# Weight sums of a Strassen stage: first set split in place, eight PSUM banks in the stage before, sums moved behind the maxima

## The chip, the cores and the metric

The kernel runs on one core of one Trainium2 chip. The metric is the device time of one execution in microseconds. Three runs of the kernel before gave 671.41, 668.84 and 676.40 us, median 671.41 us. The profile shown here is of one further execution, which took 672.27 us; its span, from the first to the last instruction, is 670.5 us, so 1.77 us of it lie outside the span.

## The reference

Three blocks follow each other: a retention attention over 4 x 8 heads, a mixture of 8 experts with top-1 routing, and a feed-forward block whose hidden layer is the maximum of three projections. The change touches only the last:

```python
def _moe2_ref(x, w1, w2, w3, w_out):          # x: 2304 x 512, w1..w3: 512 x 768, w_out: 768 x 512
    h = np.maximum(np.maximum(x @ w1, x @ w2), x @ w3)
    return (h @ w_out).astype(np.float32)
```

All data is fp32. Each product is computed as three matmuls on operands split into a high part (rounded to the fp32r format) and a low part (the rest): high x high, high x low, low x high.

## The kernel before, in words

The attention and the experts come first (0 to about 370 us). What matters here is the last block. Its input lies in SBUF as `y` (128 partitions, 4 chunks of the model dimension, 2304 tokens and a pad of 352 columns behind them). The tokens are cut into six tiles of 384. The hidden dimension is cut into six blocks of 128 (`f`). Weight unit `8E + 2f` holds w1 and w2 of a block, the next unit holds w3 and w_out, each split into high and low, in SBUF.

**The first pair of token tiles (i = 0, 1)** is done directly. `up(i, f)` runs twelve times, in the order f = 0: i = 0, 1; f = 1: i = 0, 1; and so on; call s = 2f + i. One call is three PSUM tiles (128 x 384, one each for w1, w2, w3) of twelve matmuls (L1096 to L1098). ACT copies the first tile out (L1267), DVE takes the maximum with the second (L1269) and the third (L1270), ACT rounds the result to the high part (L1271), and DVE subtracts to get the low part (L1273). A tile's bank can be written again when its reader is done. `mm_tile` hands out six banks in turn (four `mm`, and `u` and `o`), so a call's tiles take the banks of the call two before. `up` takes three callbacks: `beside[0]` is called between L1267 and L1269, `beside[1]` between L1271 and L1273, `beside[2]` behind L1273. In calls 0 to 7 they carry the decoding of the last third of the weights, which arrive as packed 64-bit words: ACT L1008 and L1009, DVE L1023 to L1037, POOL L1040 and L1041, a store to the DRAM buffer `wdec` from POOL's queue (L1043), and one step later the split into the unit (ACT L1066, DVE L1067). `down(i)` (L1454 to L1456) then multiplies the hidden tiles by w_out, three row blocks (`r`) of six `f` each; `send` copies a finished block out on ACT (L1434) and scatters it to the output from POOL's queue (L1436). `beside_down` calls a table of steps (`during`) when a row block is finished.

**The other two pairs (i = 2, 4)** use a Strassen-Winograd form of a 2 x 2 block product: seven products in place of eight, for each pair of hidden blocks (`g` = 0 to 2) and each of w1, w2, w3 (`j` = 0 to 2), so nine groups a pair of tiles (`group(q, g, j)`, q = 0 to 17). A group is seven products of six matmuls (L1470). Four of its products use sums of weight quarters, S1 to S4, as the stationary operand; the others use the weights themselves. The four sums of a group are a *set* k = 3g + j. A set is made once, during the first pair and the first groups, by these steps: `gen_load` (SP: two DMAs of 256 KB from `wdec`, L1327), `gen_sums` (DVE: four subtractions or additions of 128 x 256, L1341), `gen_high` (ACT: the high parts, one instruction of 128 x 1024, L1345), `gen_low` (DVE: the low parts, 128 x 1024, L1349, and then two stores of 512 KB to the DRAM tile `sd[k]` from SP's queue, L1353 to L1358). Where a set is worked on is its *home*: for k < 6 one of three regions of `y` whose tokens (columns 0 to 767) are already used, from set 6 on buffers of the pool `rpool`, three in number, which the output rows of `send` use as well.

The groups read the sums from nine *strips*, which are free quarters of weight units that the first pair no longer needs (`strip(n)`). `stream` loads the next strip from `sd` (SP, 256 KB, L1373); five are asked for ahead (`AHEAD`), and each group asks for four more, one behind each product that uses a strip. `form(i)` makes the right-hand operands b11, b12, b21, b22, t1 to t4 of a pair in eleven pieces of work on DVE (L1393 splits, L1398 differences) and ACT (L1386); `work(m)` does the next m of them.

The program is written in manual order: each engine executes its instructions in the order of the code, each DMA queue issues in order, and a step waits in its queue for the data it needs and for the readers of what it overwrites. The tables `gens` (steps during the `up` calls, keyed by call and callback), `during` (row blocks of `down`) and `amid` (places in the first groups) set where the steps of the sets stand in that order.

## Time and profile before

| | |
|---|---|
| three runs | 668.84, 671.41, 676.40 us |
| profiled execution | 672.27 us, span 670.5 us, mean granted TensorE clock 0.98 |
| PE busy, PEld busy | 638.2 us (95%), 598.1 us (89%) |
| DVE, ACT, POOL busy | 443.2 (66%), 275.8 (41%), 207.4 us (31%) |
| twelve `up` calls | up to 450.5 us |
| `down` of the first pair | 450.5 to 475.0 us |
| first nine groups | 475.0 to 547.1 us |

The span is the time between the first and the last instruction; times in the trace count from its start. PEld is the load of a matmul's stationary operand; a gap in PEld is where TensorE's instruction stream really stands, since the ends of pipelined matmuls are modelled. In a row with `<-`, the name behind the arrow is what ended the wait. The granted clock is 1.00 for 2.4 GHz and 0.50 for 1.2 GHz.

### The profile page before, as it was taken

How to read it: one execution, taken by the hardware profiler on the slowest of the kernel's cores; microseconds unless marked ns; L12 is line 12 of the kernel's file. 1: busy time of each engine (PE TensorE's matmuls, PEld its weight loads, DVE VectorE, ACT ScalarE, POOL GpSimd, SP SyncE). 2: the span in 40 equal slices, each digit the busy share in tenths (PEclk: the TensorE clock that was granted, in tenths of full speed). 3: DMA queues.
4: the chain of work that ended last, by engine and by line, in shares of the span. 5: the costliest groups of instructions: out<-in, count | busy, mean ns of one | idle time of the engine just before them, and what ended most of it. 6: DMA issues, size and time to landing. Idle time of an engine off the chain costs nothing.

```text
span 670.5 us, 12025 instructions
## 1 busy us (share of the span) xinstructions
PE 638.2 (95%) x4523; PEld 598.1 (89%) x4523; DVE 443.2 (66%) x866; ACT 275.8 (41%) x501; POOL 207.4 (31%) x184
## 2 busy tenths in 40 slices
PE   8999998899999999999999999999989999999994
PEld 6888877799999989898889999988889998999983
DVE  3488788455858676778877556676767677456630
ACT  3245434244645554665565533323512216211221
POOL 1001113056574644278774054511200002100011
PEclk9999989699999999999999999999989999999998
DMA  8989942335877777677865233357787641444011
GB/s 287 315 255 322 348 123 91 108 108 173 248 198 219 212 228 206 218 240 240 250 219 179 94 95 114 123 205 268 247 280 267 217 149 48 157 141 144 30 47 49
DMA packets 70548, 125.10 MB, mean 187 GB/s; under 512 B 18538, under 2 KB 41966, under 8 KB 70488
## 3 DMA queue, kind: packets, MB, share of 16 engines
q1 hardware_dynamic: 52888, 96.72, 45.3%
q0 software_dynamic: 15200, 23.45, 11.3%
q10 hardware_dynamic: 2400, 4.14, 1.7%
q8 instruction: 37, 0.61, 0.4%
q14 instruction: 23, 0.19, 0.1%
HBM read 98.32 MB, written 25.91 MB: 185 GB/s over the span
## 4 chain that ended last, share of the span: by engine, by line
PE 57%; DMA 16%; DVE 10%; issue 6%; ACT 5%; POOL 4%; ACTq 1%; SPq 0%; POOLq 0%; DVEq 0%
PE s L1470 18%; PE b L1136 10%; DMA raw<-in_weights_dram 5%; PE a L1096 3%; PE a L1098 3%; PE a L1097 3%; PE d L1456 2%; PE d L1454 2%; PE d L1455 2%; DMA wdec<-y 2%; DMA kv<-in_kv_dram 2%; DVE w L148 2%; PE xps L490 2%; DMA xr<-xd,who 1%; PE u L1096 1%
## 5 line engine op out<-in xcount | busy, mean ns | idle before, releaser
L148 DVE TENSOR_TENSOR w<-raw,w 128x1024 fp32r<-128x1024 f32 x72 | 102.0, 1418 | 45.7 <-ACT w L143 45.6
L1136 PE MATMUL b<-h,w 128*128 128x336 f32 (+7 forms) x768 | 118.7, 307 | 3.8 <-ACT h L1112 1.9
L1136 PEld LDWEIGHTS b<-h,w 128*128 128x128 f32 x768 | 109.1, 188 | 6.7 <-DVE h L1113 3.1
L143 ACT ACTIVATE w<-raw 128x1024 fp32r<-128x1024 f32 x72 | 75.9, 1055 | 29.7 <-DMA raw<-in_weights_dram 27.1
L1436 POOL DMA_INDIRECT out_dram<-o,perm_sb x18 | 20.5, 1137 | 206.3 <-ACT o L1434 165.5
L1096 PE MATMUL a<-xt,w 128*128 128x336 f32 (+7 forms) x256 | 78.7, 307 | 0.0
L1098 PE MATMUL a<-xt,w 128*128 128x336 f32 (+7 forms) x256 | 78.4, 306 | 0.0
L1097 PE MATMUL a<-xt,w 128*128 128x336 f32 (+7 forms) x256 | 78.3, 306 | 0.0
L186 POOL DMA_INDIRECT who_d<-tok,slots_i x20 | 21.0, 1050 | 95.0 <-DMA who_d<-tok,slots_i 57.6
L1096 PEld LDWEIGHTS a<-xt,w 128*128 128x128 f32 x256 | 49.1, 192 | 0.4 <-ACT xt L194 0.4
L1097 PEld LDWEIGHTS a<-xt,w 128*128 128x128 f32 x256 | 49.1, 192 | 0.0
L1098 PEld LDWEIGHTS a<-xt,w 128*128 128x128 f32 x256 | 49.0, 191 | 0.0
L173 POOL DMA_INDIRECT xr<-xd,who x24 | 37.5, 1562 | 33.2 <-DVE order_w L1157 20.9
L1096 PE MATMUL u<-ys,w 128*128 128x384 f32 x126 | 43.0, 341 | 2.8 <-ACT m L1267 1.7
L1470 PE MATMUL s<-b_ys,w 128*128 128x384 f32 x216 | 42.3, 344 | 0.2 <-ACT p L1500 0.2
L1098 PE MATMUL u<-ys,w 128*128 128x384 f32 x126 | 42.2, 335 | 0.0
L1097 PE MATMUL u<-ys,w 128*128 128x384 f32 x126 | 42.1, 335 | 0.0
L1470 PE MATMUL s<-b_xt,w 128*128 128x384 f32 x216 | 40.4, 334 | 0.0
L1470 PE MATMUL s<-b_h,w 128*128 128x384 f32 x216 | 40.4, 334 | 0.0
L1470 PEld LDWEIGHTS s<-b_ys,w 128*128 128x128 f32 x216 | 39.2, 195 | 0.7 <-ACT p L1500 0.5
L1112 ACT ACTIVATE h<-a 128x336 fp32r<-128x336 f32 (+7 forms) x64 | 26.4, 423 | 30.6 <-PE a L1098 26.9
L1040 POOL TENSOR_TENSOR d<-d,top 128x512 f32<-128x512 f32 x16 | 21.4, 1339 | 53.5 <-issue 19.7
(282 smaller groups left out, 1334.9 us busy)
## 6 DMA issues: line engine op xcount, KB each, us to landing
raw<-in_weights_dram SPq DMA_DIRECT2D x64, 512.0 KB, 5.2
w<-sd SPq DMA_DIRECT2D x72, 256.0 KB, 4.0
kv<-in_kv_dram SPq DMA_DIRECT2D x16, 512.0 KB, 6.5
qk<-in_qk_dram SPq DMA_DIRECT2D x15, 512.0 KB, 8.4
d<-in_weights_dram POOLq DMA_DIRECT2D x14, 512.0 KB, 5.7
sd<-y SPq DMA_DIRECT2D x12, 512.0 KB, 2.9
wdec<-mag POOLq DMA_DIRECT2D x16, 256.0 KB, 2.9
raw<-wdec SPq DMA_DIRECT2D x8, 512.0 KB, 3.7
```

What stands on the lines that cost most here:

```text
L143: act.activation(out=t[:, 0], in_=raws[w], func=AF.Copy)
L148: engine.tensor_tensor(out=t[:, 1], in0=raws.pop(w), in1=t[:, 0].bitcast(F32), op=ALU.subtract)
L173: pool.indirect_dma_start(out=xr[:n, r, :], out_offset=None, in_=xd[:, :], in_offset=bass.IndirectOffsetOnAxis(ap=who[:n, r, e : e + 1] if ...
L186: pool.indirect_dma_start(out=who_d[:, :], out_offset=bass.IndirectOffsetOnAxis(ap=slots_i[:L, t : t + 1], axis=0), in_=tok[:L, t : t + 1] ...
L1040: pool.tensor_tensor(out=low, in0=low, in1=top.bitcast(F32), op=ALU.mult)
L1096: pe.matmul(ps, lhsT=wh, rhs=xh, start=first, stop=False)
L1097: pe.matmul(ps, lhsT=wh, rhs=xl, start=False, stop=False)
L1098: pe.matmul(ps, lhsT=wl, rhs=xh, start=False, stop=last)
L1112: act.activation(out=h[:, 0, :wide], in_=ps, func=AF.Relu)
L1136: pe.matmul(ps, lhsT=w[:, a, f * P : (f + 1) * P], rhs=hs[f][:, b, :wide], start=(i == 0), stop=(i == len(todo) - 1),)
L1436: pool.indirect_dma_start(out=out[:, :], out_offset=bass.IndirectOffsetOnAxis(ap=perm_sb[:, g : g + 1], axis=0), in_=o, in_offset=None,)
L1470: pe.matmul(ps, lhsT=a[:, k], rhs=b[:, c], start=first and c == 0 and n == 0, stop=c == 1 and n == 2, skip_group_check=True,)
```

## The change

The `up` calls take their PSUM tiles from `any_tile`, which hands out all eight banks in turn (the two `sc` banks are new to them). Set 0 is no longer stored to DRAM and loaded again: `first_set` writes the high parts of its four sums straight into strips 0 to 3 (ACT, four of 128 x 256), then the low parts (DVE, four of 128 x 256), and `stream` skips set 0 in the first pair. For the second pair its strips are stored to `sd[0]` by four DMAs from POOL's queue. The steps of the sets move: sums that stood between the copy and the maxima of a call (`beside[0]`) stand behind the call's low part (`beside[2]`), right before the set's high and low steps. The homes are written as a table; set 6, and the high half of set 7, use `y`, among it the pad. A set's high half is stored right behind its ACT step, no longer behind the low step. The load of set 6 stands before the last pieces of `work`, that of set 7 later by one group, that of set 8 earlier by two products.

```diff
--- before.py
+++ after.py
@@ -1251,9 +1251,20 @@
         for n in (NSOON, NSOON + 1):
             dec_load(n)
 
+        bank = {"n": 0}
+
+        def any_tile(cols, name):
+            n = bank["n"] % 8
+            bank["n"] += 1
+            if n < 4:
+                return ps_m.tile([P, DM], F32, tag="mm", name=name)[:, :cols]
+            if n < 6:
+                return ps_s.tile([P, DM], F32, tag="uo"[n - 4], name=name)[:, :cols]
+            return side_tile(cols, name)
+
         def up(i, f, m, h, beside=(lambda: None,) * 3):
             wa, wb = units[8 * E + 2 * f], units[8 * E + 2 * f + 1]
-            pss = [mm_tile(TILE2, f"u{i}_{f}_{j}") for j in range(3)]
+            pss = [any_tile(TILE2, f"u{i}_{f}_{j}") for j in range(3)]
             order = [(j, c) for j in range(3) for c in range(NC)]
             if i == 0 and f == 0:
                 order.sort(key=lambda jc: jc[1])
@@ -1308,13 +1319,22 @@
             y[:, :2, span[0]].rearrange("p a (b c) -> p a b c", b=2),
             y[:, 2:, span[0]].rearrange("p a (b c) -> p a b c", b=2),
             y[:, :, span[1]].rearrange(quarters, a=2),
+            y[:, :, NTOK : NTOK + KH].rearrange(quarters, a=2),
         ]
+
+        rooms_of = {(0, 1): 0, (1, 1): 1, (2, 1): 0, (3, 1): 2, (4, 1): 1, (5, 1): 0, (6, 1): 3}
+        rooms_of.update({(1, 0): 2, (2, 0): 1, (3, 0): 0, (4, 0): 2, (5, 0): 1, (6, 0): 1, (7, 0): 3})
+
+        def stored(n):
+            if n < 2:
+                return y[:, 2 * n : 2 * n + 2, span[0]]
+            return y[:, :, span[1]] if n == 2 else y[:, :, NTOK : NTOK + KH]
         S2, S4, S3, S1 = (0, 0), (0, 1), (1, 0), (1, 1)
         gen_t = {}
 
         def gen_tile(k, low):
-            if k < NHOME:
-                return homes[(k + 2 * (1 - low)) % 3]
+            if (k, low) in rooms_of:
+                return homes[rooms_of[k, low]]
             t = rpool.tile([P, 1024], F32, tag="raw", name=f"sum{k}_{low}")
             return t.rearrange("p (a b c) -> p a b c", a=2, b=2)
 
@@ -1340,22 +1360,34 @@
             ):
                 dve.tensor_tensor(out=at(out_), in0=at(a), in1=at(b), op=op)
 
+        def gen_store(k, low):
+            to, t, n = sd[k][:, low], gen_t[k, low], rooms_of.get((k, low))
+            if n is None:
+                sp.dma_start(out=to.rearrange("p a b -> p (a b)"), in_=t.rearrange("p a b c -> p (a b c)"))
+            elif n < 2:
+                sp.dma_start(out=to.rearrange("p (a b) c -> p a (b c)", a=2), in_=stored(n))
+            else:
+                sp.dma_start(out=to, in_=stored(n))
+
+        def first_set(low):
+            for n, (a, b) in enumerate(USE):
+                src, to = gen_t[0, 1][:, a, b], strip(n)
+                if low == 0:
+                    act.activation(out=to[:, 0], in_=src, func=AF.Copy)
+                elif low == 1:
+                    dve.tensor_tensor(out=to[:, 1], in0=src, in1=to[:, 0].bitcast(F32), op=ALU.subtract)
+                else:
+                    pool.dma_start(out=sd[0][:, :, 2 * a + b], in_=to.bitcast(F32))
+
         def gen_high(k):
             t = gen_t[k, 0] = gen_tile(k, 0)
             act.activation(out=t.bitcast(F32R), in_=gen_t[k, 1], func=AF.Copy)
+            gen_store(k, 0)
 
         def gen_low(k):
-            low, high = gen_t.pop((k, 1)), gen_t.pop((k, 0))
-            dve.tensor_tensor(out=low.bitcast(F32R), in0=low, in1=high, op=ALU.subtract)
-            for half, n in ((0, (k + 2) % 3), (1, k % 3)):
-                to, t = sd[k][:, half], (high, low)[half]
-                if k >= NHOME:
-                    sp.dma_start(out=to.rearrange("p a b -> p (a b)"), in_=t.rearrange("p a b c -> p (a b c)"))
-                elif n == 2:
-                    sp.dma_start(out=to, in_=y[:, :, span[1]])
-                else:
-                    to = to.rearrange("p (a b) c -> p a (b c)", a=2)
-                    sp.dma_start(out=to, in_=y[:, 2 * n : 2 * n + 2, span[0]])
+            low = gen_t[k, 1]
+            dve.tensor_tensor(out=low.bitcast(F32R), in0=low, in1=gen_t[k, 0], op=ALU.subtract)
+            gen_store(k, 1)
 
         def strip(n):
             w, j = units[8 * E + 2 * (2 * (n // 3) + 1) + n % 3 // 2], n % 3 % 2
@@ -1368,7 +1400,7 @@
             q = streamed["n"]
             streamed["n"] += 1
             k, use = divmod(q, len(USE))
-            if k < 2 * len(sd):
+            if 0 < k < 2 * len(sd):
                 a, b = USE[use]
                 sp.dma_start(out=strip(q % NRING).bitcast(F32), in_=sd[k % len(sd)][:, :, 2 * a + b])
 
@@ -1418,16 +1450,6 @@
             ]
 
         big = {}
-        bank = {"n": 0}
-
-        def any_tile(cols, name):
-            n = bank["n"] % 8
-            bank["n"] += 1
-            if n < 4:
-                return ps_m.tile([P, DM], F32, tag="mm", name=name)[:, :cols]
-            if n < 6:
-                return ps_s.tile([P, DM], F32, tag="uo"[n - 4], name=name)[:, :cols]
-            return side_tile(cols, name)
 
         def send(i, r, ps):
             o = rpool.tile([P, 1024], F32, tag="raw", name=f"o{i}_{r}")[:, :DM]
@@ -1529,15 +1551,13 @@
             h2[i] += [new_h(i, f) for f in range(2, NFF)]
         gens = {
             (7, 2): [(gen_load, 0)],
-            (8, 0): [(gen_sums, 0)],
             (8, 1): [(gen_load, 1)],
-            (8, 2): [(gen_high, 0), (gen_low, 0)],
-            (9, 0): [(gen_sums, 1), (gen_load, 2)],
-            (9, 2): [(gen_high, 1), (gen_low, 1)],
-            (10, 0): [(gen_sums, 2), (gen_load, 3)],
-            (10, 2): [(gen_high, 2), (gen_low, 2)],
-            (11, 0): [(gen_sums, 3), (gen_load, 4)],
-            (11, 2): [(gen_high, 3), (gen_low, 3)],
+            (8, 2): [(gen_sums, 0), (first_set, 0), (first_set, 1), (gen_load, 2)],
+            (9, 2): [(gen_sums, 1), (gen_high, 1), (gen_low, 1), (first_set, 2)],
+            (10, 0): [(gen_load, 3)],
+            (10, 2): [(gen_sums, 2), (gen_high, 2), (gen_low, 2)],
+            (11, 0): [(gen_load, 4)],
+            (11, 2): [(gen_sums, 3), (gen_high, 3), (gen_low, 3)],
         }
 
         def steps(s, at):
@@ -1571,12 +1591,12 @@
 
         R3 = range(TILE2 // P)
         during = {
-            (0, 0): [(gen_sums, 4), (work, 1), (gen_load, 5)],
-            (0, 1): [(gen_high, 4), (gen_low, 4), (work, 2)],
-            (0, 2): [(gen_sums, 5), (work, 2)] + [(stream, ())] * AHEAD,
-            (1, 0): [(work, 2), (gen_high, 5), (gen_low, 5)],
-            (1, 1): [(work, 1)],
-            (1, 2): [(gen_load, 6)],
+            (0, 0): [(work, 2), (gen_load, 5)],
+            (0, 1): [(gen_sums, 4), (work, 2)],
+            (0, 2): [(gen_high, 4), (work, 1), (gen_low, 4)] + [(stream, ())] * AHEAD,
+            (1, 0): [(gen_sums, 5), (work, 2), (gen_load, 6)],
+            (1, 1): [(gen_high, 5), (work, 1), (gen_low, 5)],
+            (1, 2): [],
         }
 
         def beside_down(i):
@@ -1606,11 +1626,10 @@
         h_f += [halves(y[:, c, : 2 * TILE2]) for c in range(NC)]
         h_f += [halves(y[:, c, 2 * TILE2 : 4 * TILE2]) for c in range(2, NC)]
         amid = {
-            (0, 2): [(gen_sums, 6), (gen_load, 7)],
+            (0, 2): [(gen_sums, 6)],
             (1, 1): [(gen_high, 6)],
-            (1, 2): [(gen_low, 6)],
-            (2, 2): [(gen_sums, 7)],
-            (3, 0): [(gen_load, 8)],
+            (1, 2): [(gen_low, 6), (gen_load, 7)],
+            (2, 2): [(gen_sums, 7), (gen_load, 8)],
             (3, 1): [(gen_high, 7)],
             (3, 2): [(gen_low, 7)],
             (4, 2): [(gen_sums, 8)],
```

On DVE at call 8 (f = 4, i = 0; `m` and `y` are the running maximum, `u` the PSUM tiles, `w` a weight unit, `h` a hidden tile) the order before is:

```order
L1341 TENSOR_TENSOR y<-y 128x256 x4
L1269 TENSOR_TENSOR m_4_5107<-u_4_1_5109,m_4_5107 128x384
L1270 TENSOR_TENSOR m_4_5107<-u_4_2_5110,m_4_5107 128x384
L1067 TENSOR_TENSOR w_5091<-y,w_5091 128x512
L1273 TENSOR_TENSOR h_4_4649<-m_4_5107,h_4_4649 128x384
L1349 TENSOR_TENSOR y<-y 128x2x512
L1341 TENSOR_TENSOR y<-y 128x256 x4
L1269 TENSOR_TENSOR y<-u_4_1_5165,y 128x2x192
L1270 TENSOR_TENSOR y<-u_4_2_5166,y 128x2x192
L1273 TENSOR_TENSOR h_4_4653<-y,h_4_4653 128x384
L1349 TENSOR_TENSOR y<-y 128x2x512
```

and now:

```order
L1280 TENSOR_TENSOR m_4_5107<-u_4_1_5109,m_4_5107 128x384
L1281 TENSOR_TENSOR m_4_5107<-u_4_2_5110,m_4_5107 128x384
L1067 TENSOR_TENSOR w_5091<-y,w_5091 128x512
L1284 TENSOR_TENSOR h_4_4649<-m_4_5107,h_4_4649 128x384
L1361 TENSOR_TENSOR y<-y 128x256 x4
L1378 TENSOR_TENSOR w_4469<-y,w_4469 128x256 x2
L1378 TENSOR_TENSOR w_4516<-y,w_4516 128x256
L1378 TENSOR_TENSOR w_4615<-y,w_4615 128x256
L1280 TENSOR_TENSOR y<-u_4_1_5171,y 128x2x192
L1281 TENSOR_TENSOR y<-u_4_2_5172,y 128x2x192
L1284 TENSOR_TENSOR h_4_4653<-y,h_4_4653 128x384
L1361 TENSOR_TENSOR y<-y 128x256 x4
```

The four sums (L1341, now L1361) moved from ahead of the two maxima to behind the low part, and the four subtractions of `first_set` (L1378) stand in the place of the one large low step of set 0 (L1349).

On SP's queue, at the end of the first pair (`w` are strips, `sd_4636` is `sd[0]`, `sd_4637` is `sd[1]`, and so on), the order before is:

```order
L1373 DMA w_4469<-sd_4636 128x2x256 x2
L1373 DMA w_4516<-sd_4636 128x2x256
L1373 DMA w_4615<-sd_4636 128x2x256
L1373 DMA w_4615<-sd_4637 128x2x256
L1358 DMA sd_4641<-y 128x2x512
L1355 DMA sd_4641<-y 128x4x256
L1327 DMA sum_1_5507<-wdec 128x512 x2
L1373 DMA w_4618<-sd_4637 128x2x256
```

and now:

```order
L1405 DMA w_4615<-sd_4637 128x2x256
L1347 DMA y<-wdec 128x2x256 x2
L1368 DMA sd_4641<-y 128x2x512 x2
L1405 DMA w_4618<-sd_4637 128x2x256
```

The four loads of set 0's strips are gone, and the load of set 6 (L1327, now L1347) has moved from behind to ahead of the two stores of set 5; the next strip of set 1 (`w_4618`, strip 5) still stands behind both stores.

## Rows read from the trace of the kernel before

**Rows 1.** Waits of PEld from 360 us on: total us, times, longest us.

```profile
PEld s L1470 <- DMA w<-sd: 4.5, 2, 4.2
PEld u L1096 <- ACT m L1267: 2.3, 2, 1.4
PEld u L1096 <- DVE y L1269: 1.0, 1, 1.0
PEld u L1096 <- ACT y L1267: 1.0, 4, 0.3
PEld u L1096 <- DVE m L1269: 0.7, 1, 0.7
```

**Rows 2.** Timeline of PE: start us, busy us, engine, line, operation [idle before].

```profile
450.53 0.39 PE L1454 MATMUL d<-w,early_h 128*128 128x512 f32 x1
...
475.05 2.27 PE L1470 MATMUL s<-b_xt,w 128*128 128x384 f32 x12
...
489.01 1.33 PE L1470 MATMUL s<-b_xr,w 128*128 128x384 f32 x6 [3.92 <-DMA w<-sd]
...
496.10 2.24 PE L1470 MATMUL s<-b_xt,w 128*128 128x384 f32 x12
```

**Rows 3.** Windows: busy us of each engine, then granted clock, DMA share, GB/s.

```profile
409.00:411.00 2.00, 1.24 (x7) 1.24 (x8) 1.15 (x3) 1.24 (x4) 1.17 (x2) 1.00 0.14 39
...
491.00:492.00 1.00, 1.00 (x4) 1.00 (x4) 0.01 (x1) 0.00 (x0) 0.00 (x0) 0.50 0.85 262
```

**Rows 4.** Timeline of ACT.

```profile
429.30 0.48 ACT L1267 ACTIVATE y<-u 128x384 f32<-128x384 f32 x1
...
447.31 1.05 ACT L1345 ACTIVATE y<-y 128x1024 fp32r<-128x1024 f32 x1
```

**Rows 5.** Timeline of DVE.

```profile
435.03 3.25 DVE L1341 TENSOR_TENSOR y<-y 128x256 f32<-128x256 f32 x4 [0.58 <-DMA y<-wdec]
...
443.91 1.80 DVE L1341 TENSOR_TENSOR y<-y 128x256 f32<-128x256 f32 x4
445.63 0.55 DVE L1269 TENSOR_TENSOR y<-u,y 128x384 f32<-128x384 f32 x1
...
447.44 0.56 DVE L1273 TENSOR_TENSOR h<-y,h 128x384 fp32r<-128x384 f32 x1 [0.59 <-ACT h L1271]
448.39 1.23 DVE L1349 TENSOR_TENSOR y<-y 128x1024 fp32r<-128x1024 f32 x1 [0.39 <-ACT y L1345]
...
462.56 0.95 DVE L1393 TENSOR_TENSOR b_xt<-y,b_xt 128x768 fp32r<-128x768 f32 x1
```

**Rows 6.** Timeline of POOL and DVE around the last decode steps.

```profile
430.63 0.75 POOL L1043 DMA_DIRECT2D wdec<-y  x1 [0.30 <-DVE y L1269]
431.04 0.69 DVE L1067 TENSOR_TENSOR w<-y,w 128x512 fp32r<-128x512 f32 x1
...
435.70 1.37 POOL L1041 TENSOR_TENSOR y<-y 128x512 f32<-128x512 f32 x1
...
439.33 0.68 DVE L1067 TENSOR_TENSOR w<-y,w 128x512 fp32r<-128x512 f32 x1
```

**Rows 7.** Timeline of SP's queue (issue times).

```profile
479.48 0.36 SPq L1355 DMA_DIRECT2D sd<-y  x1
483.37 0.81 SPq L1327 DMA_DIRECT2D sum<-wdec  x2
484.23 2.58 SPq L1373 DMA_DIRECT2D w<-sd  x4
```

**Rows 8.** The chain that ended last: start us, us, what.

```profile
449.64 2.88 DMA sd<-y
...
460.95 4.81 DMA sd<-y
...
484.23 4.74 DMA w<-sd
```

**Rows 9.** All strip loads, L1373 (72 of them).

```profile
DMA to landing us min/median/max: 3.0/4.0/5.7
```

## The prediction

> **What bounds the kernel now.** I read the share of busy time first: PE issues almost all the time, so only its gaps can be won. The waits of PEld in the stretch that the change touches name them [rows 1]: 5.0 us in the `up` calls (2.3 + 1.0 + 1.0 + 0.7), where a call waits for a bank that ACT's copy or DVE's maximum of the call two before has not freed, and one of 4.2 us in the groups, for a strip. The windows show what the second costs beside the wait [rows 3]: behind those 4.2 us the granted clock is 0.50, that is 1.2 GHz; around the gap of 1.4 us at 409 us it stays at 1.00. From the strip's arrival at 489.01 to the next group at 496.10 [rows 2] are 7.1 us for five products; twelve matmuls take 2.24 with the last one's overhang, about 0.174 each, so a product of six is 1.04 and five are 5.2: clock, and 0.2 of waiting for one more strip, cost 1.9. Behind 496 us I find no gap that the change can touch.
>
> The chain says why the strip was late: SP's queue is in order [rows 7]. The load of set 6 waited for an output buffer until 483.37, the strip behind it was issued at 484.23 and landed 4.74 us later [rows 8].
>
> **The change, part by part.**
>
> *Eight banks.* A call's third tile now waits for the copy (L1267) of the call two before, and its first two tiles for the maxima of the call three before; that is two tiles, 4.2 us, more slack. The copies are held by the decode steps, which do not depend on PE and keep their times. The tightest case is the third tile of call 9. Without gaps the last `up` matmul ends at 450.5 - 5.0 = 445.5; two calls of 6.25 (36 matmuls) and a tile of 2.1 before that is 430.9, and the copy of call 7 is done at 429.8 [rows 4]: 1.1 us to spare. So `up` ends at **445.5**, 5.0 us earlier.
>
> *DVE's queue takes it back in part.* From the end of POOL's last decode step at 437.07 [rows 6] DVE is the longest queue, and I add it up, each step to the start of the next.
> - The rest of call 8 (ACT's split 0.65, DVE's 0.68, the low part 0.5) to 438.95.
> - Sums of set 0, 1.72 (443.91 to 445.63 [rows 5]; the 3.25 of the first row there ran beside POOL's last two arithmetic steps, which are over by then), to 440.7.
> - ACT's four copies of 128x256: the size is not in the trace. One lies between nothing and the 0.48 of 128x384 [rows 4]; I take 0.42, nearer to the upper row. Three run beside the sums and the last beside DVE's first subtraction; without that cover the four cost 1.7.
> - Four subtractions of 128x256: between 0.43, a sum of that size (1.72 / 4), and the 0.68 of 128x512 [rows 6]. I take 0.45, as the size is the sum's; the upper end is 0.9 more in all. To 442.5.
> - Per call, maxima and low part: 2.3 (445.63 to 447.44, and 0.47 [rows 5]). Per set: sums 1.8, ACT's high part 1.05 [rows 4] and 0.1 to hand over, low part 1.15: 4.1. Before, the maxima stood between sums and high part and hid most of ACT's 1.05 (0.39 was left [rows 5]); now DVE waits it out. That is what moving the sums behind the maxima costs.
> - So: call 9 to 444.8, set 1 to 448.9, call 10 to 451.2, set 2 to 455.3, call 11 to 457.5, set 3 to 461.6.
> - Then what `during` holds: seven splits at 0.88 and four differences at 0.96 (0.95 for one [rows 5], less or more by the overlap at the start), sums of sets 4 and 5 at 1.72, their low parts at 1.15, a wait of 0.2 for ACT: 16.0. DVE is through set 5 at **477.6**; before, the last store of set 5 was issued at 479.48 [rows 7].
>
> *PE behind it.* `down` reads the high part of call 10 in its sixth step, at 445.5 + 15 matmuls of 0.227 (108 of them from 450.53 to 475.05 [rows 2]) = 448.9. It is there 1.8 us after the first maximum of call 10 (447.44 less 445.63), at 450.65. PE waits 1.75. The groups start at 445.5 + 1.75 + 24.5 = **471.75** (475.05 before). Their operand t2 is split by 474.7 and its low part first read at 475.05: 0.3 to spare.
>
> *Set 0 in place.* Four strip loads and the wait for them fall away. Its four stores go to POOL's queue, idle until the first output row, and are read 18 groups later. The load of set 6 no longer waits for an output buffer.
>
> *The strip that was late.* Strip 5 belongs to the tenth product, at 471.75 + 9 x 1.04 = 481.1. On SP it stands behind the stores of set 5, so it is issued when DVE is through, at 477.6 + 0.45, and with its 4.74 us of before [rows 8] it is there at **482.8**: PE waits 1.7 us instead of 4.2. The ends are 3.0 and 5.7 [rows 9]; I take the row of the same strip, behind the same store. A wait of this length leaves the clock alone, as at 409 us.
>
> By the fit of the Trainium skill's page "DMA: Bandwidth & Descriptors" (section "Anatomy of one DMA"), 2.0 us and the bytes at 436 GB/s, 256 KB would be there in an estimated 2.6 us. No strip load here was that fast [rows 9]; by it the wait would vanish and the time fall by 1.7 us more.
>
> *Later strips.* Strip 13 now stands behind the low half of set 6 and the load of set 7. DVE's work in group 1 (some 8.2 us from 482.2) and the two issues (0.4 and 0.8) let it go at 491.6; with 4.74 it lands at 496.3 and is read at 482.8 + 5 x 1.04 + 7.3 + 2.1 = 497.4. About 1 us is left: the thinnest cover in the plan.
>
> **Sum.** Strip 5's product starts at 482.8 instead of 489.0: 6.2. No slow clock: 1.9, less 0.2 for the strip behind it. Together **7.9 us**. The profiled execution would take 672.27 - 7.9 = 664.4; the median of the runs shown lies 0.86 below that execution, so I predict 671.41 - 7.9 = **663.5**.
>
> **Rivals.**
> - *Stores held by the DMA engines.* ACT's high step of a set overwrites the home whose store was issued one set earlier. One store landed in 2.88 us, one took 4.81 [rows 8], and POOL's 1 MB now comes on top at 442. At 4.81 throughout, set 2's high part is 0.9 late, set 3's 1.8, later ones no more; and the strip takes 5.7 for 4.74. 2.8 less gain: 666.3. For it: a DMA share of 0.85 at 491 us [rows 3]. Against: the stretch held as many stores and loads before. Chance 0.14.
> - *POOL's stores block DVE.* A split on DVE took 0.69 while POOL issued a store, 0.68 alone [rows 6]: no blocking. If it did block, four issues of 0.75 put 3.0 us on DVE's queue: 666.5. Chance 0.05. The Trainium skill's page "SBUF — State Buffer" (section "SBUF: two separate sides") has a shared port pair, an exclusive lock between a GpSimd instruction that reads SBUF and a DVE instruction with two SBUF inputs; the sums' 3.25 beside POOL's arithmetic would be such a lock, and the pair of rows says that a DMA issue is not.
> - *The wait comes back at strips 13 and 17 (slower).* They stand behind set 6's low half and set 7's load, and behind set 8's load. If one is more than 1.1 us late, and misses by as much as strip 5 did before, it costs 4.2 and 1.9 for the clock, 6.1: 669.6. If both do, 12.2: **675.7**, slower than before. For: SP is in order and 1 us is little. Against: one store and one load of 0.5 MB stand there, and none waits for an output row. Chances 0.06 and 0.04.
> - *DVE's queue is shorter or the strip faster.* If the strip lands in 3.0, PE hardly waits for it: 661.9. If the sets never hold PE, strip 5's product starts at 445.5 + 24.5 + 9.4 = 479.4, and the gain is 9.6 + 1.9 = 11.5: 659.9. Chance 0.12.
>
> **Numbers.** My forecast, 663.5 within 2 us, has the remaining 0.59. The range 659.8 to 669.0 goes from the last rival's end to nearly the single late strip, with the dear subtractions (0.9), the strip's landing and the scatter of the runs inside. A measurement of this kernel can tell about 1% (6.7 us) from no change. Below 664.7: most of the forecast (0.43), the last rival (0.12), a little of the first (0.03): 0.58. Above 678.1: two late strips in a bad run, and what I have not seen: 0.05. Between: 0.37.
>
> **What would show it.** Right: no PEld wait in `up` above 0.3 us; the first `down` matmul near 445.5, with one wait of 1 to 2 us at its sixth step; the last store of set 5 issued near 477.6; a wait of 1 to 2 us in group 1 for a strip, the granted clock 1.00 from 480 to 500. Wrong: waits for banks left in `up` (then the banks were not the limit); stores landing in over 4 us with ACT's high steps waiting for them; a wait for a strip in groups 3 to 5 with the clock at 0.50; or the groups starting at 474 or later, which would mean that DVE's queue took back the whole gain.

## The result, and the profile after

The changed kernel takes 666.07 us, median of 22 runs (660.70 to 671.14), against 672.42 us for the kernel before on the same chip: ratio 0.9903, 95% interval 0.9876 to 0.9931. That is 6.35 us less (4.6 to 8.3 by the interval); 7.9 had been forecast. The ratio leaves out runs more than 1.5% above the fastest of their kernel, so it is not quite the quotient of the two medians. The profiled execution took 667.22 us.

The runs are a blunt measure here: the first `up` matmul, before which the change has no instruction of its own, starts between 365.2 and 377.2 us in the 14 profiles of this study. So I also compare the **stretch** from the first `up` matmul to the last matmul of the program: 661.49 - 370.82 = 290.67 us before, 656.75 - 374.09 = 282.66 us after, 8.0 less. Timeline of PE after (start us, busy us, engine, line, operation, [idle before <- what ended it]):

```profile
374.09 0.34 PE L1096 MATMUL u<-ys,w 128*128 128x384 f32 x1
...
448.98 0.39 PE L1476 MATMUL d<-w,early_h 128*128 128x512 f32 x1
...
453.30 0.50 PE L1476 MATMUL d<-w,h 128*128 128x512 f32 x1 [0.72 <-ACT h L1282]
...
474.66 0.33 PE L1492 MATMUL s<-b_xt,w 128*128 128x384 f32 x1
...
480.55 0.44 PE L1492 MATMUL s<-b_ys,w 128*128 128x384 f32 x1 [1.54 <-ACT p L1522]
...
656.75 0.39 PE L1478 MATMUL d<-w,b_h 128*128 128x512 f32 x1
```

`up` takes 74.89 us (79.71 before), `down` 25.68 (24.52), the rest 182.09 (186.44): -4.8, +1.2, -4.3. The waits of PEld from 360 us on, beside [rows 1] of before:

```profile
PEld s L1492 <- ACT p L1522: 1.9, 1, 1.9
PEld d L1476 <- ACT h L1282: 1.1, 1, 1.1
PEld s L1492 <- DMA w<-sd: 0.4, 1, 0.4
PEld d L1478 <- DVE h L1284: 0.3, 1, 0.3
```

The 5.0 us for banks are gone and so are the 4.2 us for strip 5. The last row but one is not strip 5 but strip 13, two groups later (timeline of PEld):

```profile
500.65 1.00 PEld L1492 LDWEIGHTS s<-b_xr,w 128*128 128x128 f32 x6 [0.38 <-DMA w<-sd]
```

New are 1.4 us at call 10's hidden tile (1.14 for the high part, 0.30 for the low). In group 0, `p` is late by 1.9 us: it is ACT's copy of the group's first product, and the fifth product is added to the same bank. The kernel before has a wait there too, of 0.5 us, which [rows 1] leave out (PEld):

```profile
479.59 1.00 PEld L1470 LDWEIGHTS s<-b_ys,w 128*128 128x128 f32 x6 [0.51 <-ACT p L1500]
```

ACT, DVE, SP and the chain tell why `p` is late now. ACT:

```profile
469.61 0.58 ACT L1456 ACTIVATE o<-d 128x512 f32<-128x512 f32 x1
...
479.52 0.60 ACT L1456 ACTIVATE o<-d 128x512 f32<-128x512 f32 x1 [2.17 <-DMA out_dram<-o,perm_sb]
480.02 0.48 ACT L1522 ACTIVATE p<-s 128x384 f32<-128x384 f32 x1
```

The chain that ended last:

```profile
473.08 6.34 DMA out_dram<-o,perm_sb
```

The copy of the last output block (L1456) waits until the scatter issued at 473.08 has left its buffer at 479.42, and `p`, which needs no output buffer, stands behind it. Before, it was SP's load of set 6 that stood in that line [rows 7].

That scatter started late because the scatters go one at a time. Its own copy was done at 470.19 (469.61 + 0.58), but the scatter before it landed only at 472.32 (469.08 + 3.24). The next one starts at 480.17, 0.75 us behind the landing at 479.42. POOL:

```profile
469.08 1.47 POOL L1458 DMA_INDIRECT out_dram<-o,perm_sb  x1 [3.87 <-issue]
473.08 1.31 POOL L1458 DMA_INDIRECT out_dram<-o,perm_sb  x1 [2.53 <-ACT b_ys L1418]
480.17 0.96 POOL L1458 DMA_INDIRECT out_dram<-o,perm_sb  x1 [5.78 <-ACT o L1456]
```

SP after:

```profile
473.13 0.60 SPq L1405 DMA_DIRECT2D w<-sd  x1
473.78 1.31 SPq L1347 DMA_DIRECT2D y<-wdec  x2
477.38 3.00 SPq L1368 DMA_DIRECT2D sd<-y  x2
480.44 4.90 SPq L1405 DMA_DIRECT2D w<-sd  x7
```

Set 6 is now loaded at 473.78, without a wait, and strip 5 is the first of the seven at 480.44: 106.35 us behind the first `up` matmul, against 484.23 - 370.82 = 113.41 before. DVE:

```profile
443.75 1.42 DVE L1378 TENSOR_TENSOR w<-y,w 128x256 fp32r<-128x256 f32 x4
...
450.34 1.23 DVE L1389 TENSOR_TENSOR y<-y 128x1024 fp32r<-128x1024 f32 x1 [1.18 <-ACT y L1384]
...
456.68 1.23 DVE L1389 TENSOR_TENSOR y<-y 128x1024 fp32r<-128x1024 f32 x1 [1.13 <-ACT y L1384]
...
463.07 1.22 DVE L1389 TENSOR_TENSOR y<-y 128x1024 fp32r<-128x1024 f32 x1 [1.18 <-ACT y L1384]
...
478.79 1.22 DVE L1389 TENSOR_TENSOR y<-y 128x1024 fp32r<-128x1024 f32 x1
```

Sets 1, 2 and 3 each make DVE wait some 1.15 us for ACT's high part, against 0.39 for set 1 before [rows 5]. The granted clock stays at 1.00 where it was 0.50 [rows 3]; window, columns as there:

```profile
480.00:485.00 5.00, 4.45 (x25) 4.45 (x26) 2.72 (x6) 1.38 (x4) 1.01 (x2) 1.00 0.90 307
```

### The profile page after: what moved, and what is told of

It reads as the page before. It is cut to its first block, busy times and chain, and to the rows that moved or that the text cites. A ratio compares the mean times of both kernels' runs of the same rounds, so it can differ in the third digit from the quotient of the medians.

```text
span 665.4 us, 12028 instructions
## 1 busy us (share of the span) xinstructions
PE 637.3 (96%) x4523; PEld 598.7 (90%) x4523; DVE 442.4 (66%) x869; ACT 276.8 (42%) x504; POOL 207.6 (31%) x188
## 5 line engine op out<-in xcount | busy, mean ns | idle before, releaser
L1492 PE MATMUL s<-b_ys,w 128*128 128x384 f32 x216 | 40.6, 335 | 1.5 <-ACT p L1522 1.5
L1492 PEld LDWEIGHTS s<-b_ys,w 128*128 128x128 f32 x216 | 37.7, 188 | 1.9 <-ACT p L1522 1.9
```

Of the source, the lines that this page charges most:

```text
L1492: pe.matmul(ps, lhsT=a[:, k], rhs=b[:, c], start=first and c == 0 and n == 0, stop=c == 1 and n == 2, skip_group_check=True,)
```

## The experiments

Eleven variants and the changed kernel once more, each timed beside the kernel before on the same chip. The chips differ between groups of runs (the kernel before has medians of 672.42, 673.03, 670.21 and 672.38 us on them), so compare the ratios and not the medians. Stretch, waits and rest are of one profile each. "Waits" is the sum of the gaps of PEld that its timeline marks in the stretch, "rest" the stretch less these.

| run | edit | up | down | stretch | waits | rest | median us | ratio to before, 95% interval |
|---|---|---|---|---|---|---|---|---|
| before | | 79.71 | 24.52 | 290.67 | 10.1 | 280.6 | 672.42 | 1 |
| after | the whole change | 74.89 | 25.68 | 282.66 | 3.7 | 279.0 | 666.07 | 0.9903 (0.9876 to 0.9931) |
| x1 | before, with eight banks | 75.53 | 29.80 | 290.47 | 8.5 | 282.0 | 672.33 | 0.9998 (0.9963 to 1.0033) |
| x2 | after, with six banks | 77.87 | 24.52 | 284.68 | 5.4 | 279.2 | 665.60 | 0.9896 (0.9862 to 0.9929) |
| x3 | after, set 0 through DRAM | 74.89 | 29.20 | 287.09 | 6.5 | 280.6 | 669.86 | 0.9963 (0.9928 to 0.9998) |
| x4 | after, set 6 in an output buffer | 74.89 | 25.70 | 288.11 | 6.3 | 281.8 | 671.66 | 0.9976 (0.9944 to 1.0007) |
| x5 | after, high and low apart | 74.88 | 24.52 | 280.68 | 1.4 | 279.3 | 664.24 | 0.9890 (0.9842 to 0.9938) |
| x6 | after, output halves | 74.89 | 25.42 | 281.70 | 2.6 | 279.1 | 663.21 | 0.9887 (0.9845 to 0.9929) |
| x7 | x5 and x6 | 74.89 | 24.52 | 281.10 | 1.8 | 279.3 | 662.87 | 0.9872 (0.9831 to 0.9912) |
| x8 | after, sums ahead of the maxima | 74.89 | 26.39 | 281.28 | 2.2 | 279.1 | 666.68 | 0.9897 (0.9845 to 0.9949) |
| again | after once more | 74.89 | 25.57 | 282.57 | 3.6 | 279.0 | 665.63 | 0.9898 (0.9846 to 0.9950) |
| x9 | after, `AHEAD` 8 | 74.89 | 25.82 | 282.79 | 3.8 | 279.0 | 665.82 | 0.9908 (0.9875 to 0.9940) |
| x11 | x6, `AHEAD` 8 | 74.89 | 25.60 | 282.49 | 3.5 | 279.0 | 665.37 | 0.9902 (0.9873 to 0.9930) |
| x10 | x7, `AHEAD` 8 | 74.88 | 24.52 | 280.16 | 0.8 | 279.4 | 663.82 | 0.9869 (0.9821 to 0.9916) |

The rest is 279.0 to 279.4 in ten rows, whatever the edits. It is 280.6 to 282.0 in four: before, x1, x3, x4. These four have a gap of 3 us or more with the clock at 0.50 behind it; in the other ten, no 2 us of the stretch were granted less than 0.99. So the stretch is TensorE's own 279 us, its waits, and the slow clock behind the long ones. The second profile of the changed kernel lies 0.09 us from the first in the stretch, though its first `up` matmul stands 4.4 us earlier. By the runs alone x1 and x4 are slower than the changed kernel (their intervals lie above its own), x3 nearly so; the others cannot be told from it.

### One part undone or alone

**x1, the eight banks alone.**

```diff
-            pss = [mm_tile(TILE2, f"u{i}_{f}_{j}") for j in range(3)]
+            pss = [any_tile(TILE2, f"u{i}_{f}_{j}") for j in range(3)]
...
```

(`any_tile` itself is moved ahead of `up`.)

> The kernel before with eight banks in the up calls and nothing else changed. Measure: the stretch from the first up matmul to the last matmul, 290.7 us before and 282.7 after the whole change. Theory (strip 5 sets the end of the wait in the first groups, and SP's queue sets strip 5, so PE only arrives earlier at the same wait): up loses at least 3.5 of its 5.0 us of bank waits, about 3.4 us come back at the sixth step of down (high part of call 10, which DVE's queue delivers no earlier) and the rest at the strip; stretch 289.5 to 291, time against before within 0.3%. Rival (the banks bring the gain): stretch 286 or less, 0.6% faster.

`up` is 4.2 us shorter, and nothing is gained. PEld (line numbers of before, plus 1 from `down` on and plus 11 in `up`):

```profile
447.60 0.19 PEld L1455 LDWEIGHTS d<-w,h 128*128 128x128 f32 x1 [3.59 <-ACT h L1282]
...
483.58 1.78 PEld L1471 LDWEIGHTS s<-b_xr,w 128*128 128x128 f32 x6 [3.79 <-DMA w<-sd]
```

The time saved in `up` is waited out at call 10's high part, which stands behind the sets in DVE's queue, and at strip 5, with a slow clock behind each. The windows behind them, granted clock after the busy times:

```profile
450.00:452.00 2.00, 2.00 (x6) 1.53 (x5) 1.83 (x5) 0.00 (x0) 0.00 (x0) 0.50 0.99 351
...
485.00:487.00 2.00, 2.00 (x8) 2.00 (x8) 0.56 (x1) 0.00 (x0) 0.00 (x0) 0.56 0.80 259
```

**x2, the banks undone.**

```diff
-            pss = [any_tile(TILE2, f"u{i}_{f}_{j}") for j in range(3)]
+            pss = [mm_tile(TILE2, f"u{i}_{f}_{j}") for j in range(3)]
```

> The changed kernel with six banks in the up calls. Theory (the queues of DVE and SP set the start of the groups' strips, the banks only decide where PE waits): up waits 2.5 to 3.3 us again, the waits at call 10's high part (1.1 + 0.3) and in the first groups (1.9 + 0.4) shrink by as much; stretch 282.7 to 284, no slower than the changed kernel by more than 0.2%. Rival (the banks bring the gain): stretch 286.5 to 287.5, 0.6% slower than the changed kernel.

`up` waits 3.1 us for banks again, call 10's 1.4 us go, the 1.9 at `p` become 2.1. The banks are worth 2.0 us in the stretch when the other parts are there, which lies between the theory (up to 1.3) and the rival (3.8 or more); the runs (ratio 0.9896 against 0.9903) do not show it.

**x3, set 0 by way of DRAM.**

```diff
-            (8, 2): [(gen_sums, 0), (first_set, 0), (first_set, 1), (gen_load, 2)],
-            (9, 2): [(gen_sums, 1), (gen_high, 1), (gen_low, 1), (first_set, 2)],
+            (8, 2): [(gen_sums, 0), (gen_high, 0), (gen_low, 0), (gen_load, 2)],
+            (9, 2): [(gen_sums, 1), (gen_high, 1), (gen_low, 1)],
...
```

(The cut lines give set 0's high part a home in `y` and let `stream` load set 0.)

> The changed kernel with set 0 made as the others are: high and low parts in y, stored to DRAM, its strips loaded. Theory: DVE's queue is 1.0 us longer (one wait for ACT's high part), and four strip loads and the set's stores stand on SP; stretch 1 to 2.5 us longer than 282.7. Rival (set 0 in place is where the gain comes from): strips 0 to 3 late, a wait at the first groups of 3 us or more and the clock with it, 4 us or more longer.

4.4 us longer in the stretch: the rival's size, but not its place. The products that use the first two of the four strips loaded again start 0.41 and 1.06 us late. The load of the second lands at 478.65, just ahead of its product; the landing of the first is not in the trace. 0.82 and 0.89 us are waited for strips 5 and 13. The larger part is elsewhere. ACT's first high part overwrites a region of `y` whose last decoded weights are still being stored:

```profile
441.96 1.06 ACT L1384 ACTIVATE y<-y 128x1024 fp32r<-128x1024 f32 x1 [3.65 <-DMA wdec<-y]
```

DVE then stands 2.25 us at the low part, PEld stands at call 10, and the clock falls behind it:

```profile
452.41 0.19 PEld L1476 LDWEIGHTS d<-w,h 128*128 128x128 f32 x1 [3.05 <-ACT h L1282]
```

```profile
454.00:456.00 2.00, 2.00 (x6) 1.60 (x5) 0.84 (x3) 1.30 (x2) 0.00 (x0) 0.50 0.71 246
```

The kernel before has this wait too (ACT and DVE, set 0's high and low part):

```profile
441.68 1.06 ACT L1345 ACTIVATE y<-y 128x1024 fp32r<-128x1024 f32 x1 [1.71 <-DMA wdec<-y]
...
442.77 1.23 DVE L1349 TENSOR_TENSOR y<-y 128x1024 fp32r<-128x1024 f32 x1 [2.21 <-ACT y L1345]
```

So set 0 in place saves a wait for a store, which `first_set` avoids because it writes to strips, the wait for two late strips, and 1.6 us of clock (280.6 - 279.0).

**x4, set 6 in an output buffer.**

```diff
-        rooms_of = {..., (5, 1): 0, (6, 1): 3}
+        rooms_of = {..., (5, 1): 0}
...
-            (1, 0): [(gen_sums, 5), (work, 2), (gen_load, 6)],
+            (1, 0): [(gen_sums, 5), (work, 2)],
...
-            (1, 2): [],
+            (1, 2): [(gen_load, 6)],
```

> The changed kernel with set 6 loaded again into one of the three output buffers, behind the last row block of the first pair, as before. Theory (this load's wait for an output buffer, ahead of strip 5 on SP, is what the change took away): strip 5 is issued at or after the end of a scatter, PE waits 3 us or more for it, the granted clock falls to 0.50; stretch 4 to 6 us longer than 282.7. Rival (set 5's stores, that is DVE's queue, hold strip 5 anyway): 0 to 1 us longer.

5.45 us longer: the old wait is back. SP and PEld:

```profile
473.87 3.00 SPq L1368 DMA_DIRECT2D sd<-y  x2
480.13 0.81 SPq L1347 DMA_DIRECT2D sum<-wdec  x2
480.98 4.61 SPq L1405 DMA_DIRECT2D w<-sd  x7
```

```profile
485.22 1.78 PEld L1492 LDWEIGHTS s<-b_xr,w 128*128 128x128 f32 x6 [4.24 <-DMA w<-sd]
```

This run also prices the new wait at `p`. Here it is 0.64 us, not 1.86, and the scatter that holds the buffer takes 5.10 us instead of 6.34 (chain of x4):

```profile
469.56 5.10 DMA out_dram<-o,perm_sb
```

The 1.24 us between the scatters are the 1.22 us between the waits: in the changed kernel the load of set 6 is issued 0.7 us behind this scatter and runs beside it. That the load makes the scatter longer is read from these two profiles; no run moves that load alone.

**x8, the sums ahead of the maxima again** (sets 0 to 3).

```diff
-            (8, 2): [(gen_sums, 0), (first_set, 0), (first_set, 1), (gen_load, 2)],
-            (9, 2): [(gen_sums, 1), (gen_high, 1), (gen_low, 1), (first_set, 2)],
+            (8, 0): [(gen_sums, 0)],
+            (8, 2): [(first_set, 0), (first_set, 1), (gen_load, 2)],
+            (9, 0): [(gen_sums, 1)],
+            (9, 2): [(gen_high, 1), (gen_low, 1), (first_set, 2)],
...
```

> The changed kernel with the sums of sets 0 to 3 ahead of the maxima again, as in the kernel before (set 3's sums two row blocks earlier than now). Theory A (eight banks make the place of the sums indifferent): TensorE's up work takes 74.9 to 75.6 us as now, call 10's wait stays 1 to 1.7 us or shrinks, since VectorE has set 3's sums behind it; stretch 281.5 to 283.3 us, ratio to the kernel before 0.988 to 0.992. Rival B (the sums ahead of the maxima hold the banks even with eight of them): up takes 77 us and more, stretch 284 us and more, ratio 0.994 or higher.

With eight banks `up` is not a hundredth longer. Call 10 waits 0.7 us more (with the low part 2.15, where theory A had at most 1.7), `p` and strip 13 not at all: 1.4 us less in the stretch. By the profile, sums behind the maxima cost rather than save; the runs cannot tell.

```profile
455.43 0.19 PEld L1476 LDWEIGHTS d<-w,h 128*128 128x128 f32 x1 [1.86 <-ACT h L1282]
```

DVE waits 0.39, 0.94 and 0.39 us at the three low parts and begins set 3's low part 87.2 us into the stretch instead of 89.0. ACT's high part of set 3, and behind it the copy of the first output block (462.57 in x8, 87.1 us into the stretch; 462.95 after, 88.9), come 1.8 us earlier. With it the row of scatters begins 1.8 us earlier, and the one that holds the buffer starts at 97.5 us instead of 99.0. So the wait at `p` is a late product of DVE's queue, passed on by scatters that go one at a time.

### Taking the new waits away

In the expectations of the next runs "strip 5's 0.4 us" is a mistake of mine: strip 5 does not wait in the changed kernel; the 0.4 us are strip 13's.

**x5, high and low parts of sets 1 and 2 apart.**

```diff
-            (9, 2): [(gen_sums, 1), (gen_high, 1), (gen_low, 1), (first_set, 2)],
-            (10, 0): [(gen_load, 3)],
-            (10, 2): [(gen_sums, 2), (gen_high, 2), (gen_low, 2)],
-            (11, 0): [(gen_load, 4)],
+            (9, 1): [(first_set, 2)],
+            (9, 2): [(gen_sums, 1)],
+            (10, 0): [(gen_high, 1)],
+            (10, 1): [(gen_low, 1), (gen_load, 3)],
+            (10, 2): [(gen_sums, 2)],
+            (11, 0): [(gen_high, 2)],
+            (11, 1): [(gen_low, 2), (gen_load, 4)],
```

> The changed kernel with the high and low parts of weight-sum sets 1 and 2 taken apart: the high part behind the m copy of one step, the low part a step later, so that VectorE does not wait out ScalarE's high part (in the changed kernel three waits of 1.18, 1.13 and 1.18 us, and call 10's 1.1 us and 0.3 us on TensorE behind them). Set 3 is left as it is. Theory A (VectorE's queue sets the end of the first pair's work: its three waits are what call 10 and set 5 pay): two of the three waits go, call 10's 1.4 us go or fall below 0.5 us, set 5 is stored 2 to 3.5 us earlier; the stretch from the first up matmul to the last matmul falls from 282.7 us to 280.5 to 282 us, less than the wait taken away if the 1.9 us that group 0 waits for ScalarE's p copy stay; ratio to the kernel before 0.986 to 0.989. Rival B (the waits are cover: something else, the raw sets' loads or the output copy's buffer, sets the end): VectorE's waits go, TensorE's waits in the first groups grow by as much as call 10's shrink; stretch 282.3 to 283, ratio 0.990.

Theory A: call 10 no longer waits, DVE ends set 5's low part 2.0 us earlier in the stretch, the `p` wait shrinks to 1.2, and the stretch by 2.0 us. Only one of DVE's three waits went, though. The other two are now ACT's, for a store that still reads what the high part overwrites:

```profile
446.50 1.06 ACT L1384 ACTIVATE y<-y 128x1024 fp32r<-128x1024 f32 x1 [3.56 <-DMA sd<-y]
...
451.85 1.06 ACT L1384 ACTIVATE y<-y 128x1024 fp32r<-128x1024 f32 x1 [3.87 <-DMA sd<-y]
```

**x6, output halves.**

```diff
-            o = rpool.tile([P, 1024], F32, tag="raw", name=f"o{i}_{r}")[:, :DM]
+            if i < 2:
+                n = i * 3 + r
+                if n % 2 == 0:
+                    halfway["t"] = rpool.tile([P, 1024], F32, tag="raw", name=f"o{i}_{r}")
+                o = halfway["t"][:, (n % 2) * DM : (n % 2) * DM + DM]
...
```

> The changed kernel with the first pair's six output blocks in the halves of three raw buffers instead of one buffer each, so that no output copy waits until an earlier scatter has left its buffer. What is computed is unchanged. Theory A (strip 5 still sets the end: the 1.9 us in front of the p copy and the 0.4 us at strip 5 are one wait in two places): the wait for ScalarE's p copy falls from 1.9 us to below 0.5 us, and strip 5's wait grows from 0.4 us to 1.5 to 2 us; stretch 282.2 to 282.8 us, ratio to the kernel before 0.989 to 0.991. Rival B (the output buffer is a loss of its own): the 1.9 us go and strip 5 waits 0.4 us as now; stretch 280.7 to 281 us, ratio 0.987.

Between the two theories, nearer to A: the `p` wait is gone, and strip 5, which it had covered, waits 1.16 us (lines from `send` on plus 8):

```profile
480.02 1.01 PEld L1500 LDWEIGHTS s<-b_xr,w 128*128 128x128 f32 x6 [1.16 <-DMA w<-sd]
```

**x7, both.** (The diffs of x5 and x6.)

> Both edits together: high and low parts of sets 1 and 2 taken apart, and the first pair's output blocks in halves of three buffers. Theory A (two conditions, VectorE's queue for strip 5 and the output buffer for the p copy, each of which hides the other): call 10's 1.4 us, the p copy's 1.9 us and strip 5's 0.4 us all fall to below 0.5 us each; stretch 279 to 280.3 us against 282.7 us, ratio to the kernel before 0.984 to 0.987, which is more than the two edits give one by one. Rival B: the strips' landing (4 us and more, six loads at once) sets strip 5 whatever the issue: strip 5 waits 1.5 us or more, stretch 281 to 282 us, ratio 0.988 to 0.989.

Neither theory: call 10 and `p` wait no longer, but strips 5 and 13 do, 0.69 and 0.66 us, and 0.47 us of issue follow. The stretch is 0.4 us longer than with x5 alone.

**The changed kernel again.** (No edit.)

> The changed kernel once more, as the measure for the three others of this group of runs. Expected: a stretch from the first up matmul to the last matmul of 282.7 us, made of 279.0 us of TensorE's own time and 3.7 us of waits (call 10's 1.4, the p copy's 1.9, strip 5's 0.4), and a ratio to the kernel before of 0.988 to 0.992. If the waits of this second profile differ by more than 0.5 us, the comparisons of single profiles are no better than that.

Waits 3.6 us and stretch 282.57: as far as one pair of profiles can show, differences of a few tenths count, in the stretch.

**x9, `AHEAD` 8 in the changed kernel.**

```diff
-AHEAD = 5
+AHEAD = 8
```

> The changed kernel with AHEAD 8 instead of 5: all four strips of set 1 are loaded right behind set 4's stores, ahead of set 5's two stores in SP's queue, which wait for VectorE's low part. Theory A (strip 5 is late only because of the place of its load): strip 5's 0.4 us go, and the p copy still waits for the output buffer, 1.9 us or up to 1 us longer since three more loads of 256 KB run beside the scatter; stretch 282.2 to 283.2 us, ratio 0.988 to 0.992. Rival B (the three loads delay raw set 6 or the scatter by more than they save): p wait 3 us and more, stretch 284 us.

No gain, no loss. Strip 13's wait is gone, and DVE's add waits in its place (below).

**x11, x6 with `AHEAD` 8.**

```diff
-AHEAD = 5
+AHEAD = 8
```

> The output halves (no output copy waits for a scatter) with AHEAD 8. Theory A (strip 5's 1.2 us of the run with the halves alone come from the place of its load behind set 5's stores): they go, and call 10's 1.2 us stay; stretch 280.2 to 280.6 us, ratio 0.984 to 0.988. Rival B (the loads' landing under a full DMA sets it): strips still wait 1 us or more, stretch 281.5 us or more.

Both theories fell: strip 5 waits no longer, as A had it, but the stretch grows by 0.8 us over x6; B's stretch came without its wait for strips. DVE, PEld and the chain of x11:

```profile
484.11 0.56 DVE L1521 TENSOR_TENSOR y<-y 128x384 f32<-128x384 f32 x1 [5.46 <-DMA sd<-y]
```

```profile
485.01 0.99 PEld L1500 LDWEIGHTS s<-b_ys,w 128*128 128x128 f32 x6 [1.34 <-ACT p L1530]
487.83 1.01 PEld L1500 LDWEIGHTS s<-b_h,w 128*128 128x128 f32 x6 [0.76 <-DVE y L1537]
```

```profile
477.74 6.24 DMA sd<-y
```

A store of set 5, issued behind three more strip loads, takes 6.24 us (median of the L1368 stores in the changed kernel from 464 to 500 us: 4.0), and the groups' results go to the part of `y` that it reads. The wait went from the strip to the store.

**x10, x7 with `AHEAD` 8.**

```diff
-AHEAD = 5
+AHEAD = 8
```

> High and low parts of sets 1 and 2 taken apart, output halves, and AHEAD 8. Theory A (with the strips' place mended nothing in the first groups waits): stretch 279.0 to 279.5 us, ratio 0.982 to 0.986, the fastest of all. Rival B (landing under a full DMA): the waits at strips 5 and 13 or 17 stay, 1 us or more in sum; stretch 280.2 us or more, ratio 0.986 to 0.989.

The shortest stretch, 280.16 us, with one wait left; 0.7 us above theory A, by that same store (481.09, 5.86 us):

```profile
490.80 1.01 PEld L1500 LDWEIGHTS s<-b_h,w 128*128 128x128 f32 x6 [0.78 <-DVE y L1537]
```

By the runs 0.9869 against 0.9903 and 0.9898 for the changed kernel: the same direction, but the intervals overlap. That it is faster than the changed kernel is shown in the stretch (2.5 us), not in the time of whole runs.

## Why the prediction was right, and where it was not

**The sum.** 7.9 us were forecast and 8.0 came in the stretch; the runs' 6.35 agree within their interval (4.6 to 8.3). The median of 666.07 is 2.6 above the 663.5 forecast, just outside "within 2 us": 1.0 of it because the kernel before has a median of 672.42 here and not 671.41, the rest because the runs show 6.35 and not 7.9. The total is right, but its parts did not all come as said, and it took luck. Of the five signs that were to show it right, four came; a wait for a strip in group 1 did not.

- *`up` 5.0 us shorter*: 4.82, no bank wait left. Right.
- *Four subtractions at 0.45 us*: four from 443.75 to the next step at 445.09, 0.34 each, below the lower end of 0.43; an error of 0.5. POOL's stores, the first issued at 444.46 beside them, did not slow them.
- *DVE waits out ACT's high part, 1.05 a set*: 1.13 to 1.18, three times. Right; x8, with 0.39, 0.94 and 0.39, shows that the place of the sums is the cause.
- *PE waits 1.75 for call 10's high part*: 1.14 and 0.30 for the low part. Right in place, 0.3 too long.
- *DVE through set 5 at 477.6*: 478.79 + 1.22 = 480.01, which is 476.7 in times of before (first `up` matmul 3.27 earlier). 0.9 early.
- *Strip 5 waits 1.7 without loss of clock*: it did not wait at all. **This is the step that failed.** The text said that the load of set 6 no longer waits for an output buffer. True, but the buffer was still late, and I did not ask who needs it next: the copy of the last output block, with `p` behind it in ACT's queue. The sum puts `p` at nothing: it counts nine products of 1.04 from the start of the groups without a gap, and leaves out the 0.51 us at `p` that the kernel before had. `p` cost 1.86 us and covered strip 5; x6 takes it away and finds strip 5's 1.16 us, 0.5 below my figure, as DVE was early. 1.86 and 0.38 (strip 13) stand where 1.7 stood: a wait that was counted and did not come, and one that came and was not counted, nearly cancel. That the sum held here was luck.
- *Strip 13 has about 1 us to spare*: it waited 0.38. DVE let go at 493.83, 490.6 in times of before, as reckoned (491.6 less the 1.2 of issues), and the load took 4.73 us for my 4.74; but set 6's store and set 7's two loads ahead of it on SP took 2.0 us to issue instead of 1.2. The chain:

```profile
493.84 0.37 SPq L1370
...
494.31 0.51 SPq L1347
...
494.91 0.87 SPq L1347
...
495.88 4.73 DMA w<-sd
```

- *The clock's 1.9 us*: back. Before, 290.67 less 10.1 of waits is 280.6, 1.6 above the 279.0 of after; the forecast had 1.7 (1.9 less 0.2 of waiting). Right.

**What the parts are worth.** The eight banks stood first in my account. Alone they gain 0.2 us in the stretch (x1), at the end 2.0 (x2). Set 0 in place is worth 4.4 (x3) and set 6 in `y` 5.45 (x4), the moved sums -1.4 (x8): together 10.5, more than the 8.0 of the whole, because the parts need each other: with one of them missing, TensorE stands at another queue and the rest gain less. I put nothing beside "set 0 in place" but four strip loads; most of what it saved was a wait of ACT for a store of decoded weights, and the clock behind it. Not undone one by one are the later steps of sets 4 and 5 in `during`, the earlier store of the high halves and the places of sets 7 and 8, so what they are worth is not shown. Set 4's low part waited 3.46 us for ACT's high part before (DVE, 466.96) and does not wait after.

**Rivals.** Stores held by the DMA engines make no high step wait in the changed kernel, where those steps wait for DVE; they did in x5, in ACT's rows. Of the late strips 13 and 17 only 13 came, with 0.38 us and without the slow clock. That the sets never hold PE is what x5, x7 and x10 come near to: the forecast of that rival was 11.5 us of gain, x10 has 10.5.

## What to carry to other kernels

When a change takes away a wait for a shared buffer, ask which engine's queue holds the next request for that buffer, and what stands behind it that needs no buffer: the wait moves there. Ask also what the buffer's present holder waits for: here a scatter had to let the one before it land. Sum the gaps of the bounding engine before and after and look at what is left over: here 279 us of work, the waits and the slow clock account for every variant, and a part's worth is what the stretch loses without it, not the wait that it removes by itself. Where an untouched part scatters by more than the effect, compare a stretch that begins behind it, and profile one kernel twice to know how far that can be trusted.

## What the runs showed of the hardware

The granted clock fell to 0.50 behind gaps of TensorE of 3.05 us (x3), 3.59 and 3.79 (x1) and 4.24 (x4, before), and stayed at 1.00 behind 1.86 us (after) and 2.08 us (x2). It cost 1.6 us in x3 and before, 3.0 for the two gaps of x1 and 2.8 in x4 (rest less 279.0). In x4 the granted clock reads 0.50 from 485 to 491 us, in the others for one stretch of 2 us behind a gap and 0.74 to 0.91 on either side of it. Why the same gap of 4.24 us cost more in x4 than before stays open.

An output scatter took 5.10 us in x4 and 6.34 after, with set 6's two loads of 256 KB issued 0.7 us behind it; a store of 512 KB took 6.24 us with three more strip loads ahead of it, against a median of 4.0; a strip load in x7 took 7.24 (chain, 488.71). The output scatters ran one at a time: in the changed kernel each starts 0.75 to 0.77 us behind the landing of the one before. In x9, x10 and x11, loads asked for earlier moved a wait from strips to a store. The estimate that the prediction took from the Trainium skill's page "DMA: Bandwidth & Descriptors" (section "Anatomy of one DMA"), 2.6 us for 256 KB, was not reached by any strip load whose landing the traces have: the fastest took 2.94 (x3), before 3.0 [rows 9]. The page measured that fit on DMAs from GpSimd's queue, and these loads are SP's; the DMA share is 0.90 to 0.97 in the 5 us stretches in which strips load in the changed kernel (480 to 490 and 495 to 500 us).

The four sums of a set took DVE 1.79 us in the changed kernel and 3.89 in x8, where set 0's stand beside POOL's last arithmetic steps again, as in [rows 5]:

```profile
438.80 3.89 DVE L1361 TENSOR_TENSOR y<-y 128x256 f32<-128x256 f32 x4
```

The Trainium skill's page "SBUF — State Buffer" (section "SBUF: two separate sides") has a shared port pair that a GpSimd instruction that reads SBUF and a DVE instruction with two SBUF inputs lock against each other. The trace agrees: in x8 POOL's two TENSOR_TENSOR run from 438.56 to 441.49, beside the sums.
